# A decode block on one core: Tile's scheduling replaced by a hand-made plan of waits, Tile's closing part moved to the front, and weights kept on TensorE

## The chip, the cores and the metric

The kernel runs on one core of one Trainium2 chip. The metric is the device time of one execution in microseconds (us); less is better. Engines are named as the profile names them: PE (matmuls; PEld its weight loads), DVE, ACT, POOL, SP. SP computes nothing here; it only issues DMAs, in the order of its program, and a wait on SP holds everything behind it. All times are from one profiled execution unless another source is named.

## What is computed

One token x (1024 values) goes through a layer norm to xn. From xn come two branches, and x is added to their sum:

```python
xn = layernorm(x)
q = (xn @ wq)                       # 1024 x 4096: 32 heads of 128
k, v = last 4096 positions of the caches, 4 key heads, each shared by 8 query heads
o = softmax(q @ k.T / sqrt(128)) @ v
h = gelu(layernorm(xn) @ w1 + b1)   # 1024 x 3584
out = x + o @ wo + h @ w2 + b2      # wo 4096 x 1024, w2 3584 x 1024
```

All inputs are bf16. Nothing is used twice, so the work is reading some 40 MB from memory: K 4.2, wq 8.4, w1 7.3, V 4.2, w2 7.3, wo 8.4.

## The kernel before, in words

Everything large passes through four SBUF slots of 32 KB per partition (the ring, L63 to L68; `slots` says who lives where). Slot 0 holds K, then the second half of w1, then the first half of wo. Slot 1 holds the first half of wq, then the first half of w1, then the second half of w2. Slot 2 holds the second half of wq, then V, then the second half of wo. Slot 3 holds the transposed K as scratch (kt_scr), then the first half of w2.

SP issues the large loads in one fixed order: K in four loads, one for each key head (L75), wq in two (L94), w1 in two (L208), V in three (L214: two heads, one, one), w2 in two (L222), wo in six (L230: 16 rows at once, then 8, 4, 2, 1, 1), and at the end half of the output (L369). ACT issues the small ones: x, b2, b1 (L81 to L85), and the other half of the output (L370). A load into a slot waits until the slot's former tenant has been read: for the first half of w1 these are the matmuls of wq's first half (L239), for its second half DVE's transposes of K (L192), for V the matmuls of wq's second half, for w2's first half the copies out of kt_scr (L199, L202), for wo's second half the matmuls with V (L321).

Tile, a library, sets the semaphores: each engine's program is written in the order of the code, except where Tile's scheduler moves an instruction, and an instruction waits for those semaphores that its operands call for. At the end Tile adds a closing part: drains, barriers of all engines and the clearing of semaphores.

The stages: x is brought onto 128 partitions by eight small matmuls (L126) and normalised twice (L129 to L173), mostly on DVE, giving xnT and yT. DVE transposes K in 32 x 32 blocks (L192), and ACT (24 copies, L199) and DVE (10, L202) put the blocks in their places in kT. PE multiplies xnT with wq (L239) into eight rows, one to a column group and bank, and each matmul loads its weights again; q is transposed (L263) and put into a block matrix qm (L268); scores (L277), their maximum (L285 to L296), Exp on ACT (L299), a transpose to eTb (L301), and 32 matmuls with V into o_all (L321). In between stand the matmuls of w1 (L259) and Gelu (L314), whose result is transposed to hT (L316). Then w2's and wo's rows are summed into accf (L340), the halves of a row in two column groups in turn; x, b2 and b1 came into the sums as matmuls with one row (L181, L183, L251). The last four rows of wo (the tail, L354 to L364) go to accumulators of their own; DVE and ACT add the parts (L366, L367) and the output leaves on two queues.

Of the kernel before, what the change touches and what calls it, by code (L numbers as in the profile page):

```python
# [8 lines left out]
FP32 = mybir.dt.float32  # L9
BF16 = mybir.dt.bfloat16  # L10
ACT = mybir.ActivationFunctionType
ALU = mybir.AluOpType
AX = mybir.AxisListType


@with_exitstack
def kernel(
# [38 lines left out]
    consts = ctx.enter_context(tc.tile_pool(name="consts", bufs=1))  # L56
    small = ctx.enter_context(tc.tile_pool(name="small", bufs=2))
    ring = ctx.enter_context(tc.tile_pool(name="ring", bufs=1))
    ps_acc = ctx.enter_context(tc.tile_pool(name="ps_acc", bufs=1, space=bass.MemoryType.PSUM))
    ps_tp = ctx.enter_context(tc.tile_pool(name="ps_tp", bufs=1, space=bass.MemoryType.PSUM))  # L60
    ps_f = ctx.enter_context(tc.tile_pool(name="ps_f", bufs=2, space=bass.MemoryType.PSUM))

    RING_ELEMS = 16384  # L63

    slots = {"k_sb": 0, "wq0": 1, "wq1": 2, "kt_scr": 3, "w10": 1, "w11": 0, "v_sb": 2, "w20": 3, "w21": 1, "wo0": 0, "wo1": 2}

    def ring_tile(name):
        return ring.tile([P, RING_ELEMS], BF16, tag=f"ring{slots[name]}", name=name, align_bytes=256)  # L68

    x_flat = A_x.rearrange("a b d -> (a b d)")  # L70


    k_sb = ring_tile("k_sb")
    for g in range(Hkv):
        nc.sync.dma_start(out=k_sb[g:P - Hkv + g + 1:Hkv, :], in_=A_k_cache[0, g, Sk - W:Sk, :].rearrange("(r c) d -> r (c d)", r=P // Hkv))  # L75
    mhalf = consts.tile([P, 1], FP32)
    nc.vector.memset(mhalf[:], -0.5)
    dummy = consts.tile([1, 2], FP32)
    nc.scalar.activation(out=dummy[:, 0:1], in_=mhalf[0:1, 0:1], func=ACT.Exp)
    x_row = consts.tile([1, D], BF16)  # L80
    nc.scalar.dma_start(out=x_row[:].rearrange("a (s n) -> a s n", s=16), in_=x_flat.rearrange("(a s n) -> a s n", a=1, s=16))  # L81
    b2_row = consts.tile([1, D], BF16)
    nc.scalar.dma_start(out=b2_row[:].rearrange("a (s n) -> a s n", s=16), in_=B_b2.rearrange("(a s n) -> a s n", a=1, s=16))
    b1_row = consts.tile([1, Fd], BF16)
    nc.scalar.dma_start(out=b1_row[:].rearrange("a (s n) -> a s n", s=16), in_=B_b1.rearrange("(a s n) -> a s n", a=1, s=16))  # L85


    wq_tiles, w1_tiles = [], []
    wq_v = A_wq.rearrange("(p c) n -> p c n", p=P)
    w1_v = B_w1.rearrange("(p c) n -> p c n", p=P)  # L90
    for i in range(2):
        t = ring_tile(f"wq{i}")
        tv = t[:].rearrange("p (r n) -> p r n", r=4)
        nc.sync.dma_start(out=tv, in_=wq_v[:, 4 * i:4 * i + 4, :])  # L94
        wq_tiles.append(tv)
    kt_scr = ring_tile("kt_scr")


    ident = consts.tile([P, P], BF16)
    make_identity(nc, ident[:])  # L100
    ident_f = consts.tile([P, P], FP32)
    make_identity(nc, ident_f[:])
    ones_f = consts.tile([P, P], FP32)
    nc.vector.memset(ones_f[:], 1.0)
    sel4 = consts.tile([P, Hq], FP32)
    ones_bf = consts.tile([P, 1], BF16)
    nc.vector.memset(ones_bf[:], 1.0)
    qm = consts.tile([P, Hkv, Hq], BF16)
    nc.gpsimd.memset(qm[:], 0.0)

    spread = consts.tile([Hq, 4, P], BF16)
    nc.gpsimd.memset(spread[:], 0.0)
    nc.gpsimd.affine_select(out=spread[:], in_=spread[:], compare_op=ALU.not_equal, fill=1.0, base=0,
                            pattern=[[-1, 4], [1, P]], channel_multiplier=-4)

    gmask = consts.tile([Hq, Hkv], FP32)
    nc.gpsimd.memset(gmask[:], 1.0)
    nc.gpsimd.affine_select(out=gmask[:], in_=gmask[:], compare_op=ALU.is_ge, fill=0.0, base=0,
                            pattern=[[-REP, Hkv]], channel_multiplier=1)
    nc.gpsimd.affine_select(out=gmask[:], in_=gmask[:], compare_op=ALU.is_ge, fill=0.0, base=REP - 1,  # L120
                            pattern=[[REP, Hkv]], channel_multiplier=-1)

    xf = consts.tile([P, C], FP32)
    x_ps = ps_f.tile([P, C], FP32, tag="pf", name="x_ps")
    for c in range(C):
        nc.tensor.matmul(x_ps[:, c:c + 1], lhsT=x_row[0:1, c:D:C], rhs=ones_bf[0:1, 0:1], start=True, stop=True)  # L126
    nc.vector.tensor_copy(out=xf[:], in_=x_ps[:])

    def layernorm(src_f32, dst_f32, dst_bf):  # L129
        n = float(P * C)  # L130
        st = small.tile([P, 1], FP32, tag="ln_st")
        nc.vector.reduce_sum(out=st[:], in_=src_f32, axis=AX.X)
        tot = ps_f.tile([P, 1], FP32, tag="pf", name="ln_tot")
        nc.tensor.matmul(tot[:], lhsT=ones_f[:], rhs=st[:], start=True, stop=True)
        negmean = small.tile([P, 1], FP32, tag="ln_nm")
        nc.vector.tensor_scalar_mul(out=negmean[:], in0=tot[:], scalar1=-1.0 / n)
        xc = small.tile([P, C], FP32, tag="ln_xc")
        nc.vector.tensor_scalar(out=xc[:], in0=src_f32, scalar1=negmean[:], scalar2=None, op0=ALU.add)
        sq = small.tile([P, C], FP32, tag="ln_sq")
        st2 = small.tile([P, 1], FP32, tag="ln_st2")  # L140
        nc.vector.tensor_tensor(out=sq[:], in0=xc[:], in1=xc[:], op=ALU.mult)
        nc.vector.reduce_sum(out=st2[:], in_=sq[:], axis=AX.X)
        tot2 = ps_f.tile([P, 1], FP32, tag="pf", name="ln_tot2")
        nc.tensor.matmul(tot2[:], lhsT=ones_f[:], rhs=st2[:], start=True, stop=True)
        ve = small.tile([P, 1], FP32, tag="ln_ve")
        nc.vector.tensor_scalar(out=ve[:], in0=tot2[:], scalar1=1.0 / n, scalar2=eps, op0=ALU.mult, op1=ALU.add)
        rstd = small.tile([P, 1], FP32, tag="ln_rstd")
        nc.gpsimd.tensor_tensor(out=rstd[:], in0=ve[:], in1=mhalf[:], op=ALU.pow)
        nc.vector.tensor_scalar_mul(out=dst_f32, in0=xc[:], scalar1=rstd[:])
        nc.vector.tensor_copy(out=dst_bf, in_=dst_f32)  # L150

    xn_f = consts.tile([P, C], FP32)
    xnT = consts.tile([P, C], BF16)
    layernorm(xf[:], xn_f[:], xnT[:])
    n_el = float(P * C)
    st12 = small.tile([P, 2], FP32, tag="ln2_st")
    nc.vector.reduce_sum(out=st12[:, 0:1], in_=xn_f[:], axis=AX.X)
    sq2 = small.tile([P, C], FP32, tag="ln2_sq")
    nc.vector.tensor_tensor(out=sq2[:], in0=xn_f[:], in1=xn_f[:], op=ALU.mult)
    nc.vector.reduce_sum(out=st12[:, 1:2], in_=sq2[:], axis=AX.X)  # L160
    tot12 = ps_f.tile([P, 2], FP32, tag="pf", name="ln2_tot")
    nc.tensor.matmul(tot12[:], lhsT=ones_f[:], rhs=st12[:], start=True, stop=True)
    mean2 = small.tile([P, 1], FP32, tag="ln2_mean")
    nc.vector.tensor_scalar_mul(out=mean2[:], in0=tot12[:, 0:1], scalar1=1.0 / n_el)
    msq2 = small.tile([P, 1], FP32, tag="ln2_msq")
    nc.vector.tensor_tensor(out=msq2[:], in0=mean2[:], in1=mean2[:], op=ALU.mult)
    ve2 = small.tile([P, 1], FP32, tag="ln2_ve")
    nc.vector.tensor_scalar(out=ve2[:], in0=tot12[:, 1:2], scalar1=1.0 / n_el, scalar2=eps, op0=ALU.mult, op1=ALU.add)
    nc.vector.tensor_tensor(out=ve2[:], in0=ve2[:], in1=msq2[:], op=ALU.subtract)
    rstd2 = small.tile([P, 1], FP32, tag="ln2_rstd")  # L170
    nc.gpsimd.tensor_tensor(out=rstd2[:], in0=ve2[:], in1=mhalf[:], op=ALU.pow)
    yT = consts.tile([P, C], BF16)
    nc.vector.tensor_scalar(out=yT[:], in0=xn_f[:], scalar1=mean2[:], scalar2=rstd2[:], op0=ALU.subtract, op1=ALU.mult)  # L173

    accf = ps_acc.tile([P, 512], FP32, tag="accf")
    accq = ps_acc.tile([P, 2, 512], FP32, tag="accq", name="accq")
    nc.vector.memset(accq[:], 0.0)
    nc.vector.memset(accf[:], 0.0)
    for half in range(2):
        pr = 32 * half  # L180
        nc.tensor.matmul(accf[pr:pr + 1, :], lhsT=ones_bf[0:1, 0:1], rhs=x_row[0:1, 512 * half:512 * half + 512],  # L181
                         start=True, stop=False, tile_position=(0, pr))
        nc.tensor.matmul(accf[pr:pr + 1, :], lhsT=ones_bf[0:1, 0:1], rhs=b2_row[0:1, 512 * half:512 * half + 512],  # L183
                         start=False, stop=False, tile_position=(0, pr))


    NS = 4
# [213 lines left out]
```

## Time and profile before

| what | value |
| --- | --- |
| median of 3 runs (lowest, highest) | 102.19 us (102.12, 102.35) |
| the profiled execution | 102.22 us |
| its span, first to last instruction | 100.5 us |
| busy: PE, DVE, ACT, POOL | 48%, 46%, 32%, 4% of the span |
| weight loads on PE (beside the matmuls) | 18.7 us in 367 instructions |
| read from memory | 39.86 MB, 397 GB/s over the span |
| SP's queue q1, share of 16 DMA engines | 93.3% |

Times on lines of the profile are us from the start of the span, durations us or, where it says so, ns. The DMA row cuts the span into 40 slices of 2.5 us; each digit is the busy share of the sixteen DMA engines in tenths. The chain is followed back from the last instruction, at each step to what released it. An answer by windows gives, for each stretch, its length, the busy time of PE, PEld, DVE, ACT and POOL with the number of instructions, the granted PE clock, the DMA share and GB/s. A packet's record can fall into one slice as a whole, so single short stretches can show a share over 1.

### The profile page before, as it was taken

What the parts mean: (1) busy time and instruction counts of PE and PEld (TensorE: products, weight loads), DVE (VectorE), ACT (ScalarE), POOL (GpSimd) and SP (SyncE); (2) the same over time, 40 slices, a digit from 0 to 9 for tenths busy, and PEclk for the clock granted to TensorE, in tenths of its full rate; (3) what the DMA queues carried; (4) which work ended last, traced back from release to release, by engine and by line L of the source; (5) the groups of instructions that cost most, each with busy time, mean ns of one, the idle gap of its engine ahead of it and who ended that gap; (6) DMA issues with size and microseconds to landing.
All of it is one profiled execution on the core that took longest, in us unless ns stands there. A gap on an engine that the chain in (4) does not pass through costs nothing.

```text
span 100.5 us, 945 instructions
## 1 busy us (share of the span) xinstructions
PE 48.1 (48%) x367; PEld 18.7 (19%) x367; DVE 45.9 (46%) x64; ACT 32.1 (32%) x35; POOL 3.8 (4%) x16
## 2 busy tenths in 40 slices
PE   1565000007600930048937347991920993199780
PEld 1222000002100300024303213431400230033220
DVE  5654169999999999951234336008100000000011
ACT  4100000899999999940020472000000000000020
POOL 6033000000000000000000000000000000000000
PEclk9999999999999997555799999999997559759999
DMA  5699999999999899999999999999999999999910
GB/s 157 262 420 417 443 430 509 483 417 417 417 430 391 388 497 388 445 445 388 403 421 434 421 505 399 471 395 434 445 434 425 417 443 404 430 408 412 388 51 1
DMA packets 2494, 39.92 MB, mean 397 GB/s; under 512 B 309, under 2 KB 311, under 8 KB 698
## 3 DMA queue, kind: packets, MB, share of 16 engines
q1 hardware_dynamic: 2482, 39.85, 93.3%
q8 instruction: 3, 0.05, 0.2%
q10 hardware_dynamic: 8, 0.01, 0.0%
q14 instruction: 1, 0.01, 0.0%
HBM read 39.86 MB, written 0.00 MB: 397 GB/s over the span
## 4 chain that ended last, share of the span: by engine, by line
DMA 79%; PE 12%; SPq 5%; issue 1%; DVE 0%
DMA wq<-in_A_wq_dram 29%; DMA wo<-in_A_wo_dram 27%; DMA v_sb<-in_A_v_cache_dram 24%; PE o_all L321 7%; PE accq L239 3%; SPq L75 2%; PE acc_a L354 1%; SPq L214 1%; SPq L230 1%; SPq L94 1%; DVE res L366 0%; PE acc_b L363 0%; PE acc_b L358 0%
## 5 line engine op out<-in xcount | busy, mean ns | idle before, releaser
L199 ACT COPY kT<-kt_scr 32x1024 bf16<-32x1024 bf16 x24 | 25.0, 1042 | 15.5 <-DVE kt_scr L192 15.2
L192 DVE STREAM_TRANSPOSE kt_scr<-k_sb 128x4096 bf16<-128x4096 bf16 x4 | 17.4, 4413 | 3.1 <-DMA k_sb<-in_A_k_cache_dram 3.1
L239 PE MATMUL accq<-wq,xnT 128*1 128x512 bf16 x64 | 6.8, 601 | 20.3 <-DMA wq<-in_A_wq_dram 20.3
L202 DVE COPY kT<-kt_scr 32x4096 bf16<-32x4096 bf16 x10 | 12.2, 1219 | 0.2
L348 DVE COPY bulk_b<-accf 33x192 f32<-33x192 f32 x1 | 0.3, 350 | 25.1 <-PE accf L340 25.1
L349 ACT COPY bulk_a<-accf 33x320 f32<-33x320 f32 x1 | 0.4, 419 | 35.4 <-DVE bulk_b L348 35.4
L340 PE MATMUL accf<-w,hT 128*1 128x512 bf16 x56 | 9.0, 492 | 4.5 <-DMA w<-in_B_w_dram 4.5
L340 PE MATMUL accf<-wo,o 128*1 128x512 bf16 x56 | 7.8, 433 | 4.4 <-DMA wo<-in_A_wo_dram 4.4
L321 PE MATMUL o_all<-v_sb,eTb 128*32 128x512 bf16 x32 | 7.1, 379 | 2.1 <-DMA v_sb<-in_A_v_cache_dram 2.1
L239 PEld LDWEIGHTS <-xnT 128*1 128x1 bf16 x64 | 2.1, 116 | 24.6 <-issue 24.6
L277 PE MATMUL sp<-kT,qm 128*32 128x512 bf16 x32 | 5.6, 878 | 0.4 <-DVE qm L268 0.4
L263 PE MATMUL qT_ps<-ident,q_sb 128*128 128x128 bf16 x8 | 1.2, 308 | 8.0 <-DVE q_sb L242 8.0
L340 PEld LDWEIGHTS <-hT 128*1 128x1 bf16 x56 | 2.9, 102 | 10.1 <-issue 8.4
L340 PEld LDWEIGHTS <-o 128*1 128x1 bf16 x56 | 2.7, 92 | 9.6 <-issue 7.3
L321 PEld LDWEIGHTS <-eTb 128*32 128x32 bf16 x32 | 3.0, 97 | 6.1 <-issue 2.5
L259 PE MATMUL acch<-w,yT 128*1 128x448 bf16 x64 | 3.4, 352 | 0.0
L324 DVE TENSOR_TENSOR o_m<-o_all,grs 32x512 f32<-32x512 f32 x1 | 0.7, 678 | 5.3 <-PE o_all L321 5.3
L316 DVE STREAM_TRANSPOSE hT<-h_sb 128x896 bf16<-128x896 bf16 x1 | 1.7, 1720 | 2.4 <-ACT h_sb L314 2.4
L282 ACT COPY sc<-sp 128x512 f32<-128x512 f32 x1 | 0.6, 586 | 6.6 <-PE sp L277 6.6
L277 PEld LDWEIGHTS <-qm 128*32 128x32 bf16 x32 | 2.1, 149 | 3.1 <-issue 3.1
L280 DVE COPY sc<-sp 128x512 f32<-128x512 f32 x1 | 0.7, 692 | 3.7 <-PE sp L277 3.7
L299 ACT ACTIVATE e<-sc,nmx 128x1024 bf16<-128x1024 f32 x1 | 1.1, 1147 | 3.9 <-DVE nmx L296 3.9
(93 smaller groups left out, 38.6 us busy)
## 6 DMA issues: line engine op xcount, KB each, us to landing
w<-in_B_w_dram SPq DMA_DIRECT2D x4, 3584.0 KB, 15.7
wq<-in_A_wq_dram SPq DMA_DIRECT2D x2, 4096.0 KB
k_sb<-in_A_k_cache_dram SPq DMA_DIRECT2D x4, 1024.0 KB, 7.2
wo<-in_A_wo_dram SPq DMA_DIRECT2D x1, 4096.0 KB
v_sb<-in_A_v_cache_dram SPq DMA_DIRECT2D x1, 2048.0 KB
v_sb<-in_A_v_cache_dram SPq DMA_DIRECT2D x2, 1024.0 KB, 22.7
wo<-in_A_wo_dram SPq DMA_DIRECT2D x1, 2048.0 KB, 24.4
wo<-in_A_wo_dram SPq DMA_DIRECT2D x1, 1024.0 KB
```

The lines of the kernel that those rows point to most:

```text
L75: nc.sync.dma_start(out=k_sb[g:P - Hkv + g + 1:Hkv, :], in_=A_k_cache[0, g, Sk - W:Sk, :].rearrange("(r c) d -> r (c d)", r=P // Hkv))
L192: nc.vector.transpose(out=scr[:, s, :], in_=k2[:, s, :])
L199: nc.scalar.copy(out=kT[32 * Cd:32 * Cd + 32, R, s, :].rearrange("p (c j) -> p c j", j=32), in_=T5[32 * R:32 * R + 32, s, :, Cd, :])
L202: nc.vector.tensor_copy(out=kT[32 * Cd:32 * Cd + 32, R, :, :].rearrange("p s (c j) -> p (s c) j", j=32), in_=kt_scr[32 * R:32 * R + 32, :] ...
L239: nc.tensor.matmul(accq[32 * t:32 * t + 1, b, :], lhsT=xnT[:, c:c + 1], rhs=w3[:, r, j * 512:(j + 1) * 512], start=(c == 0), stop=(c == C ...
L259: nc.tensor.matmul(acch[32 * t:32 * t + 1, b, :NH], lhsT=yT[:, c:c + 1], rhs=w3[:, r, j * NH:(j + 1) * NH], start=False, stop=(c == C - 1) ...
L263: nc.tensor.transpose(qT_ps[:, b * 4 + hh, :], q_sb[:, b, hh * Dh:(hh + 1) * Dh], ident[:])
L277: nc.tensor.matmul(sp[32 * R:32 * R + 32, :].rearrange("p (b r u) -> p b u r", r=8, u=4), lhsT=qm[:, g, :], rhs=kv, start=(g == 0), stop=( ...
L299: nc.scalar.activation(out=e128[:], in_=sc[:], func=ACT.Exp, bias=nmx[:], scale=scale, accum_out=l_loc[:])
L316: nc.vector.transpose(out=hT[:], in_=h_sb[:].rearrange("p (d c) -> p c d", c=CW2))
L321: nc.tensor.matmul(o_all[:].rearrange("h g d -> h (g d)"), lhsT=eTb[:, 32 * c:32 * c + 32], rhs=v4[:, :, c, :], start=(c == 0), stop=(c == ...
L340: nc.tensor.matmul(accf[32 * half:32 * half + 1, :], lhsT=vec[kind](c), rhs=wap[:, half * 512:(half + 1) * 512], start=False, stop=(idx == ...
```

## The change

The kernel is written again without Tile's pools and scheduler. A class Plan collects the operations with the keys that each reads and writes, works out who must wait for whom, and writes waits and semaphores itself. Only the first two loads of K are issued inside Tile's part; then that part is closed, with its drains, barriers and clearing, and all that follows stands behind it. At the end POOL waits for the two output DMAs and clears the semaphores used.

Weights: `ldw` loads a weight and `mm` multiplies without loading, so that one load serves several matmuls. For wq and w1 a row's weight is loaded into four column groups and used for eight matmuls; for w2 it is loaded once, into the first column group, and used for both halves of the row (accumulator accw). wo keeps two column groups in turn.

Further: x is loaded as 32 rows of 32 and brought onto 128 partitions by four matmuls; b1, x and b2 are loaded across partitions (b1x, x2, b2x) after POOL has cleared those tiles and are added on DVE (xb, h_pre, base); q is transposed against a matrix of four columns; the first half of w1 is multiplied before the scores and the second half after the maximum; Gelu is one activation, with its table load placed right behind Exp; bulk_a moves from ACT to DVE. The slots, the sizes of the large loads and their order on SP are as before.

The core of the diff; the rest renames tiles and adds the keys:

```diff
-    small = ctx.enter_context(tc.tile_pool(name="small", bufs=2))
-    ring = ctx.enter_context(tc.tile_pool(name="ring", bufs=1))
-    ps_acc = ctx.enter_context(tc.tile_pool(name="ps_acc", bufs=1, space=bass.MemoryType.PSUM))
-    ps_tp = ctx.enter_context(tc.tile_pool(name="ps_tp", bufs=1, space=bass.MemoryType.PSUM))
-    ps_f = ctx.enter_context(tc.tile_pool(name="ps_f", bufs=2, space=bass.MemoryType.PSUM))
...
+class Plan:
+    def __init__(self, nc):
+        self.nc = nc
+        self.engines = {"pe": nc.tensor, "dve": nc.vector, "act": nc.scalar, "pool": nc.gpsimd, "sp": nc.sync}
+        self.ops = []
+    def add(self, eng, fn, r=(), w=(), dma=None):
+        self.ops.append((eng, fn, tuple(r), tuple(w), dma))
+
+    def emit(self, done):
+        nc, ops = self.nc, self.ops
+        writer, readers, deps = {}, {}, []
+        for n, (eng, fn, r, w, dma) in enumerate(ops):
+            need = set()
+            for k in r:
+                if k in writer:
+                    need.add((writer[k], True))
+            for k in w:
+                if k in writer:
+                    need.add((writer[k], True))
+                need.update((m, False) for m in readers.get(k, ()))
+            keep = set()
+            for m, after_write in need:
+                if m == n:
+                    continue
+                same = ops[m][0] == eng and ops[m][4] is None and dma is None
+                if same and (eng == "pe" or not after_write):
+                    continue
+                keep.add(m)
+            deps.append(keep)
+            for k in r:
+                readers.setdefault(k, []).append(n)
+            for k in w:
+                writer[k] = n
...
+        for n, (eng, fn, r, w, dma) in enumerate(ops):
+            e, lanes = self.engines[eng], {}
+            for m in waits[n]:
+                s, v = value[m]
+                if id(s) not in lanes or lanes[id(s)][1] < v:
+                    lanes[id(s)] = (s, v)
+            for s, v in lanes.values():
+                e.wait_ge(s, v)
+            i = fn()
+            if dma is not None:
+                if dma is True:
+                    dma = nc.alloc_semaphore(f"dma{n}")
+                    i.then_inc(dma, 16)
+                value[n] = (dma, 16)
+                used.append(dma)
+            elif n in wanted:
+                ticks[eng] += 1
+                i.then_inc(sems[eng], 1)
+                value[n] = (sems[eng], ticks[eng])
+        last = [value[m] for m in done]
+        for s, v in last:
+            nc.gpsimd.wait_ge(s, v)
+        nc.clear_and_free_semaphores(used)
...
-    k_sb = ring_tile("k_sb")
-    for g in range(Hkv):
-        nc.sync.dma_start(out=k_sb[g:P - Hkv + g + 1:Hkv, :], in_=A_k_cache[0, g, Sk - W:Sk, :].rearrange("(r c) d -> r (c d)", r=P // Hkv))
+    k_sem = [nc.alloc_semaphore(f"k{g}") for g in range(Hkv)]
+
+    def load_k(g):
+        return nc.sync.dma_start(out=k_sb[g:P - Hkv + g + 1:Hkv, :],
+                                 in_=A_k_cache[0, g, Sk - W:Sk, :].rearrange("(r c) d -> r (c d)", r=P // Hkv)).then_inc(k_sem[g], 16)
+
+    for g in range(2):
+        tc.no_tile_sem_insts.add(load_k(g).ins.name)
+    tc.close()
+    tc.compile()
...
+    def dma(eng, out_ap, in_ap, r=(), w=()):
+        q = plan.engines[eng]
+        plan.add(eng, lambda: q.dma_start(out=out_ap, in_=in_ap), r, w, True)
+    def ldw(w_ap, pos, r):
+        def go():
+            with nc.discard():
+                i = pe.ldweights(w_ap, tile_position=pos).ins
+            return pe.add_instruction(mybir.InstLdweights(
+                name=nc.get_next_instruction_name(), engine=i.engine, tile_size=(P, 32), tile_position=pos, ins=i.ins, outs=i.outs))
+        op("pe", go, r, ())
...
+    def mm(out_ap, w_ap, x_ap, start, stop, pos, r, w):
+        def go():
+            with nc.discard():
+                i = pe.matmul(out_ap, lhsT=w_ap, rhs=x_ap, start=start, stop=stop, tile_position=pos).ins
+            return pe.add_instruction(mybir.InstMatmult(
+                name=nc.get_next_instruction_name(), engine=i.engine, start_tensor_calc=start, stop_tensor_calc=stop,
+                tile_size=i.tile_size, tile_position=i.tile_position, ins=i.ins, outs=i.outs, ldweights=False))
+        op("pe", go, r, w)
...
+    for g in range(2):
+        plan.add("sp", lambda: None, (), (f"k{g}", "slot0"), k_sem[g])
+    for g in range(2, 4):
+        plan.add("sp", lambda g=g: load_k(g), (), (f"k{g}",), k_sem[g])
+    for i in range(2):
+        dma("sp", wq_t[i], wq_v[:, 4 * i:4 * i + 4, :], (), (f"wq{i}", f"slot{1 + i}"))
...
-    x_row = consts.tile([1, D], BF16)
-    nc.scalar.dma_start(out=x_row[:].rearrange("a (s n) -> a s n", s=16), in_=x_flat.rearrange("(a s n) -> a s n", a=1, s=16))
+    x32 = sb("x32", [Hq, Hq], BF16)
+    dma("act", x32, x_flat.rearrange("(a j) -> a j", a=Hq), (), ("x32",))
+    for name, t in (("x2", x2), ("b2x", b2x), ("b1x", b1x)):
+        op("pool", lambda t=t: pool.memset(t, 0.0), (), (name,))
+    dma("act", b1x[0:97:32, :], B_b1.rearrange("(t n) -> t n", t=4), (), ("b1x",))
+    dma("act", x2[0:33:32, :], x_flat.rearrange("(t n) -> t n", t=2), (), ("x2",))
+    dma("act", b2x[0:33:32, :], B_b2.rearrange("(t n) -> t n", t=2), (), ("b2x",))
...
+    for u in range(4):
+        mm32(x_ps, spread[:, u, :], x32[:, 8 * u:8 * u + 8], u == 0, u == 3, ("spread", "x32"), ("misc",))
...
+    xb = sb("xb", [33, 512], FP32)
+    op("dve", lambda: dve.tensor_tensor(out=xb, in0=x2, in1=b2x, op=ALU.add), ("x2", "b2x"), ("xb",))
...
-            for j in range(NJQ):
-                b, t = divmod(j, 4)
-                nc.tensor.matmul(accq[32 * t:32 * t + 1, b, :], lhsT=xnT[:, c:c + 1], rhs=w3[:, r, j * 512:(j + 1) * 512],
-                                 start=(c == 0), stop=(c == C - 1), tile_position=(0, 32 * t))
+            c = 4 * i + r
+            for t in range(4):
+                ldw(xnT[:, c:c + 1], (0, 32 * t), ("xnT",))
+            for b in range(2):
+                for t in range(4):
+                    j = 4 * b + t
+                    mm(acc2[32 * t:32 * t + 1, b, :], xnT[:, c:c + 1], wq_t[i][:, r, j * 512:(j + 1) * 512],
+                       c == 0, c == C - 1, (0, 32 * t), (f"wq{i}", f"slot{1 + i}"), ("acc2",))
+    dma("sp", w1_t[0], w1_v[:, 0:4, :], (), ("w10", "slot1"))
+    dma("sp", w1_t[1], w1_v[:, 4:8, :], (), ("w11", "slot0"))
-    v_sb = ring_tile("v_sb")
-    v4 = v_sb[:].rearrange("p (g c d) -> p g c d", g=Hkv, c=NCH)
-    for g0, g1 in ((0, 2), (2, 3), (3, 4)):
-        src = A_v_cache[0, g0:g1, Sk - W:Sk, :].rearrange("g (p c) d -> p g c d", p=P)
-        nc.sync.dma_start(out=v4[:, g0:g1, :, :], in_=src)
+    for g0, g1 in ((0, 2), (2, 3), (3, 4)):
+        dma("sp", v4[:, g0:g1, :, :], A_v_cache[0, g0:g1, Sk - W:Sk, :].rearrange("g (p c) d -> p g c d", p=P), (), (f"v{g0}", "slot2"))
...
-    for b in range(2):
-        for hh in range(4):
-            nc.tensor.transpose(qT_ps[:, b * 4 + hh, :], q_sb[:, b, hh * Dh:(hh + 1) * Dh], ident[:])
+    w1_part(0)
+            mm32(qT_ps[:, k, :], blk, selq, True, True, (f"q_sb{b}", "selq"), ("qo",))
...
+    dma("sp", slot[3][:, :14 * D].rearrange("p (r n) -> p r n", r=14), w2_v[:, 0:14, :], kt_keys, ("w20", "scr0", "scr1", "scr2", "scr3"))
+    dma("sp", slot[1][:, :14 * D].rearrange("p (r n) -> p r n", r=14), w2_v[:, 14:28, :], (), ("w21", "slot1"))
...
+    w1_part(1)
...
+    op("act", lambda: act.activation(out=dummy[:, 1:2], in_=mhalf[0:1, 0:1], func=ACT.Gelu_apprx_tanh), ("mhalf",), ("act_warm",))
...
-    for b in range(2):
-        nc.scalar.activation(out=h_sb[:, b * NH:(b + 1) * NH], in_=acch[:, b, :NH], func=ACT.Gelu_apprx_tanh, bias=zcol[:])
+    op("dve", lambda: dve.tensor_tensor(out=h_pre, in0=acc2[:, :, :NH], in1=b1x.rearrange("p (b n) -> p b n", b=2), op=ALU.add), ("acc2", "b1x"), ("h_pre",))
+    h_sb = sb("h_sb", [P, 2 * NH], BF16)
+    op("act", lambda: act.activation(out=h_sb, in_=h_pre.rearrange("p b n -> p (b n)"), func=ACT.Gelu_apprx_tanh), ("h_pre",), ("h_sb",))
...
-        for a, b in zip(cuts[:-1], cuts[1:]):
-            nc.sync.dma_start(out=tv[:, a:b, :], in_=wo_v[:, nr * i + a:nr * i + b, :])
+    wo_t = [slot[s].rearrange("p (r n) -> p r n", r=16) for s in (0, 2)]
+    dma("sp", wo_t[0], wo_v[:, 0:16, :], (), ("wo0", "slot0"))
+    cuts = [0, 8, 12, 14, 15, 16]
+    for a, b in zip(cuts[:-1], cuts[1:]):
+        dma("sp", wo_t[1][:, a:b, :], wo_v[:, 16 + a:16 + b, :], (), (f"wo1{a}", "slot2"))
...
-    for idx, (kind, c, wap) in enumerate(chunk_src[:n_bulk]):
-        for half in range(2):
-            nc.tensor.matmul(accf[32 * half:32 * half + 1, :], lhsT=vec[kind](c), rhs=wap[:, half * 512:(half + 1) * 512],
-                             start=False, stop=(idx == n_bulk - 1), tile_position=(0, 32 * half))
+    for c in range(CW2):
+        i, r = divmod(c, 14)
+        wap = slot[3 - 2 * i][:, r * D:(r + 1) * D]
+        ldw(hT[:, c, 0:1], (0, 0), ("hT",))
+        for half in range(2):
+            mm(accw[0:1, half, :], hT[:, c, 0:1], wap[:, 512 * half:512 * half + 512], c == 0, c == CW2 - 1, (0, 0), (f"w2{i}",), ("accw",))
+    for half in range(2):
+        op("dve", lambda half=half: dve.tensor_copy(out=base[32 * half:32 * half + 1, :], in_=accw[0:1, half, :]), ("accw",), ("base",))
+    op("dve", lambda: dve.tensor_tensor(out=base, in0=base, in1=xb, op=ALU.add), ("base", "xb"), ("base",))
...
+    for c in range(n_bulk):
+        wap, key = wo_row(c)
+        for half in range(2):
+            ldw(o8[:, c:c + 1], (0, 32 * half), ("o8",))
+            mm(accf[32 * half:32 * half + 1, :], o8[:, c:c + 1], wap[:, 512 * half:512 * half + 512],
+               c == 0, c == n_bulk - 1, (0, 32 * half), (key,), ("qo",))
...
-    out_v = out.rearrange("a b (t s n) -> t (a b) s n", t=2, s=16)
-    nc.sync.dma_start(out=out_v[0], in_=res[0:1, :].rearrange("a (s n) -> a s n", s=16))
-    nc.scalar.dma_start(out=out_v[1], in_=res[32:33, :].rearrange("a (s n) -> a s n", s=16))
+    out_v = out.rearrange("a b (t s n) -> t (a b) s n", t=2, s=16)
+    dma("sp", out_v[0], res[0:1, :].rearrange("a (s n) -> a s n", s=16), ("res_a", "res_b"), ("out0",))
+    dma("act", out_v[1], res[32:33, :].rearrange("a (s n) -> a s n", s=16), ("res_a", "res_b"), ("out1",))
+    plan.emit([len(plan.ops) - 2, len(plan.ops) - 1])
```

## The prediction

> **What bounds the kernel now.** I read the page's DMA row and queue table first, then the chain of work that ended last, then the timeline where that chain changes hands. The DMA row, the queue table and the head of the chain:
>
> ```profile
> DMA  5699999999999899999999999999999999999910
> ...
> q1 hardware_dynamic: 2482, 39.85, 93.3%
> ...
> DMA 79%; PE 12%; SPq 5%; issue 1%; DVE 0%
> ```
>
> SP's queue q1 carries all 39.85 MB, and from the third slice to the last but two the sixteen DMA engines are never idle. The chain in order of time says the same: its three long pieces are transfers, and what stands between them (PE L239, PE L321) only sets when SP may issue, long before the queue runs dry.
>
> ```profile
> 4.05 28.77 DMA wq<-in_A_wq_dram
> ...
> 37.08 23.69 DMA v_sb<-in_A_v_cache_dram
> ...
> 68.85 27.22 DMA wo<-in_A_wo_dram
> ```
>
> So the rule for this kernel: compute is free until it delays an issue past the point where the queue empties, and every microsecond in which q1 is empty is added to the end. The windows answer gives the full rate (last number of a row: GB/s):
>
> ```profile
> 33.00:60.80 27.80, 13.81 (x141) 5.77 (x133) 15.62 (x26) 14.96 (x17) 0.00 (x0) 0.82 1.01 431
> 60.80:92.00 31.20, 20.69 (x122) 7.78 (x124) 4.30 (x7) 0.12 (x1) 0.00 (x0) 0.84 1.00 427
> ```
>
> At that rate 1 MiB takes 2.45 us. What an empty queue costs can be read at the start, the only place where it is empty. SP issues K's first load at 0.79; nothing moves until 2.0:
>
> ```profile
> 1.50:2.00 0.50, 0.00 (x0) 0.00 (x0) 0.50 (x1) 0.50 (x1) 0.50 (x3) 1.00 0.01 4
> 2.00:2.50 0.50, 0.38 (x6) 0.39 (x7) 0.44 (x2) 0.50 (x1) 0.38 (x2) 1.00 2.98 786
> ```
>
> and in the answer for tile k_sb:
>
> ```profile
> DMA to landing us min/median/max: 5.3/7.2/9.0
> ```
>
> K's first load landed 5.3 after its issue (at 6.1), though 1 MiB needs 2.45 when it follows another: K's fourth load is in at 13.5 (DVE's first transpose starts at 13.57), so loads two to four took (13.5-6.1)/3 = 2.47 each. An empty queue cost 5.3-2.45 = 2.85. The small end: x_row, 2 KB, issued at 0.79, lets PE start at 2.11, 1.3 later; the output's 1 KB, issued at 98.41, is seen by SP at 99.69, again 1.3.
>
> **The change part by part.** One profiled execution took 102.22 (span 100.5 and 1.7 around it); the median of the three runs is 102.19, so the sum needs no correction.
>
> *SP's waits.* This decides. In the new code a DMA that writes a key already written waits for that writer, and a DMA counts as written when it has landed. The three loads of V all write "slot2", and so do the five pieces of wo's second half. The built program's list for SP confirms it: V's second and third load wait for the landing of the load before, and wo's second to fifth piece likewise; before, none of these six waited. SP works in order, so behind such a wait everything still to come is unissued: at V w2 and wo, at wo the rest of wo and the output. The queue therefore really drains, six times. Each time costs: SP wakes (0.05), issue to first data, first data's latency, last data to landing, less what a transfer in a full queue costs anyway. No row shows a drained queue in mid-kernel; from below it is 1.3 (x_row, the output: one small row each), from above 0.05+2.85 = 2.9 (K's first load). The three 1 MiB transfers (V twice, wo's second piece) are nearest to K's load, but that one ran beside the start of everything else: the trace's landing records put its first engine at 5.57, its last at 6.08, so 2.3 to 2.8 over the steady time. I take 2.4. The three small pieces (0.5, 0.25, 0.25 MiB) lie between the ends; I take 1.9. Sum 3 x 2.4 + 3 x 1.9 = **12.9**; ends 7.8 and 17.4.
>
> The Trainium skill, "DMA: Bandwidth & Descriptors", section "Anatomy of one DMA", gives a fixed cost of about 2.0 us per DMA besides bytes/436 GB/s (fitted for another issue path), nearly all of it the wait for the write's receipt. That speaks against this change: six receipts become visible, 6 x 2.0 = 12.0 as an estimate, for 114.0 in place of the total below. The rows here bracket it (1.3 and 2.85).
>
> *K.* The new program books K's first two loads as two writers of slot0, so SP also waits for the first before issuing the third. That happens at 6.1; behind it wait K's last two loads and wq. The second load is in flight until about 8.6 (6.1+2.47), and 6.15+1.3 = 7.45 brings the third's first data before that. Cover holds but barely: 0.3 (0 to 0.7).
>
> *Tile's closing part, run early.* Its drains, barriers and clearing stood between the output's landing (99.69) and the span's end (100.5), 0.8. There remain two waits on POOL and a clear; SP's like steps take 0.06 each, the clear 0.1: 0.25. **-0.55** (-0.8 to -0.3). At the front the same 0.7 comes after SP's two K issues (end 1.97), so the other engines start at 2.7, not 0.8. x then queues behind K's data: b2's row, issued at 1.40, landed at 5.9, 4.5 later, so x lands by 7.2 instead of 2.1. From xf's copy (3.75) to yT (10.5) the chain takes 6.7; with x's matmuls 0.7 and sel4 and xb ahead of the transposes (some 1.0, by L193's 0.36 and L366's 0.48) DVE starts them at 15.6 instead of 13.57. The cover: DVE's copies end at 45.4 instead of 43.4; the first w1 load, issued at 26.8, lands only at 42.5, and the second is issued when the transposes end, 33 instead of 31, so q1 stays full. eTb is ready at 60.4 instead of 58.3, and V's last load now lands at 65.6. Cost 0; were V on time at 60.8, still 0.
>
> *TensorE.* Weight loads fall from eight to four per row of wq and w1, and from two to one per row of w2; they overlap matmuls and all lie in stretches where PE waits for data afterwards (L239 idle 20.3 for wq). Worth 0. w2 now puts both halves into one column group. Before, alternate groups gave 28 matmuls in 3.19; in one group PV gives 32 in 7.07, 0.221 each. 56 x 0.221 = 12.4 in place of 9, beside 21 us of transfers of wo. Cost 0 unless the clock is at half all along (rival). w1's first half before the scores, bias and x+b2 added on DVE, one Gelu with its table load ahead: all between 45 and 75, where q1 has w2 and wo queued. 0. SP's queue order is unchanged, so no transfer is moved past another.
>
> *Tail.* From the last landing to the output's issue 1.0 as before.
>
> Sum: 102.22 + 12.9 + 0.3 - 0.55 = **114.9**.
>
> **The rivals.**
> - *Cheap restart*: all six cost 1.3, by x_row and the output: 102.22+7.8-0.55+0.3 = 109.8. For: receipt and issue are the same for any size. Against: sixteen engines must all be in, and K's load shows over 2.3.
> - *Dear restart*: 2.9 each and K 0.7: 102.22+17.4+0.7-0.55 = 119.8. Against: K's load is also the program's first.
> - *PE becomes the bound*: with the clock at 0.5 throughout w2 takes 25 us. Its second half then ends near 100 and 56 matmuls of wo (0.2 each) near 111, past wo's landing, so about 1.5 on top: 116.4. The page shows 0.5 only in three spells of some 3 to 10 us, so it is unlikely.
> - *Late front*: if the new jump after the closing part stalls SP past 6.1, K's third load comes late one for one; 1 to 2 us gives 116 to 117. For it, no row; the one jump before (to the program's body) shows no gap, 0.79 follows the barrier's release at 0.72. The Trainium skill, "Runtime: NRT & Kernel Launch", section "Instruction fetch mechanics", says that a taken branch out of the fetched window waits for a fetch; no run here shows it, and SP has 3.4 us of cover.
> - *Not slower*: DMA engines catch up after a pause, so that bytes and not the queue set the time. Place: the stretch behind each landing. Price: the waits vanish, 102.22-0.55 = 101.7. It decides from a rate behind a pause of more than twice the steady one. Against: after the cold start K ran at 2.47 per MiB, no faster than later. That the waits are not in the program is excluded by its list.
>
> **How the numbers follow.** Forecast (average restart 1.6 to 2.6) 0.62; cheap 0.15; dear 0.11; PE 0.05; late front 0.04; not slower 0.03. The range leaves out the last and the far end of dear: 109.3 to 118.5. A difference of 0.2% (102.0 to 102.4) is about what a measurement of this kernel can tell from no change; faster 0.02, same 0.01, slower 0.97.
>
> **What would show it.** In the profile after: idle slices in the DMA row near 57, 62 and four times in the last 14 us; SP waiting for DMA v_sb and wo, each wait as long as the transfer it follows; V's third load landing near 65 to 66; out issued near 111; span end 0.3 instead of 0.8 behind the output's landing; DVE's transposes at about 15.6. Wrong it would be if the DMA row stays full between 55 and 66, or if pieces of wo land 0.6 to 1.2 apart as now.

## The result and the profile after

The changed kernel takes 117.79 us (median of 4 runs, 117.57 to 118.08) against 102.2 before: a ratio of 1.1525, 95% interval 1.1496 to 1.1555. The forecast of 114.9 had the sign and the place; the time lies 2.9 above it, inside the range. In some executions the chip is in a slower state and a kernel takes over 1.5% longer than its fastest execution; those are left out of every time and ratio below.

The page of the profile after (the profiled execution took 118.08, its span is 116.3): the DMA row, SP's queue, and the chain by engine.

```profile
DMA  4998989989899999997184999989999994366320
...
q1 hardware_dynamic: 2482, 39.85, 83.0%
...
DMA 85%; PE 11%; SPq 1%; issue 0%; DVE 0%
```

The same 39.85 MB now fill 83.0% of a longer span. A slice is 2.9 us here. The row dips twice: "7184" from 52 to 64, where V is loaded, and "4366320" in the last 20 us, where wo's last pieces are. The chain in order of time (start, length, what) shows what stands there:

```profile
36.80 20.02 DMA slot<-in_A_v_cache_dram
56.82 0.02 issue
56.83 4.78 DMA slot<-in_A_v_cache_dram
61.62 0.02 issue
61.63 4.69 DMA slot<-in_A_v_cache_dram
66.32 0.04 issue
66.36 8.53 PE qo_ps L188 x32
74.89 0.02 issue
74.91 24.92 DMA slot<-in_A_wo_dram
99.83 0.02 issue
99.85 4.71 DMA slot<-in_A_wo_dram
104.56 0.02 issue
104.58 3.57 DMA slot<-in_A_wo_dram
108.14 0.02 issue
108.16 2.62 DMA slot<-in_A_wo_dram
110.78 0.02 issue
110.80 2.71 DMA slot<-in_A_wo_dram
113.51 0.04 issue
```

Each DMA row runs from the issue of a load to its landing. Where "0.02 issue" and the next DMA row follow, SP issued the next load only after that landing. Before, these loads stood in the queue one behind the other. SP's own waits say it by name (engine, line, releaser: us in total, times, longest):

```profile
SPq L174 <- DMA slot<-in_A_wo_dram: 34.5, 4, 24.6
SPq L174 <- DMA slot<-in_A_v_cache_dram: 24.1, 2, 19.6
```

Each of the six rows holds its transfer (2.45 for 1 MiB at the rate of before, 1.23 for 0.5, 0.61 for 0.25) and a gap:

| load that waited | issue to landing | transfer | gap |
| --- | --- | --- | --- |
| V, third head | 4.78 | 2.45 | 2.33 |
| V, fourth head | 4.69 | 2.45 | 2.24 |
| wo, 4 rows | 4.71 | 2.45 | 2.26 |
| wo, 2 rows | 3.57 | 1.23 | 2.34 |
| wo, 1 row | 2.62 | 0.61 | 2.01 |
| wo, last row | 2.71 | 0.61 | 2.10 |

Together 13.3, and 0.02 each for SP to wake: 13.4.

Where the whole difference of the two spans (116.3 - 100.5 = 15.8) came in can be followed along the landings (from the chains above and in the prediction, and from the trace's landing records):

| point | before | after | later by | of it new |
| --- | --- | --- | --- | --- |
| wq complete, PE goes on | 32.87 | 33.18 | 0.3 | 0.3 |
| V's first load landed | 55.89 | 56.82 | 0.9 | 0.6 |
| V complete | 60.77 | 66.32 | 5.55 | 4.6 |
| wo, first piece of the second half | 92.40 | 99.83 | 7.4 | 1.9 |
| wo complete | 97.36 | 113.51 | 16.15 | 8.7 |
| end of the span | 100.5 | 116.3 | 15.8 | -0.4 |

4.6 and 8.7 are the six gaps. The 0.3 is K's wait, the -0.4 the shorter end. What the prediction has no term for are the 0.6 and the 1.9: at these two points no transfer is new, yet the load that SP waits for is late. The DMA view of the window 97 to 99 shows one of them (forty slices of 50 ns):

```profile
DMA  7977777000000090000000000000000000000000
...
q8 instruction: 1, 0.02, 3.2%
```

The view books a packet where it starts: the last data packets start at 97.32 and take 0.61. One engine then fetches 16 KB of program code (queue q8, the lone 9 at 97.7; it takes 1.01), and SP, which waits for all sixteen engines, goes on at 99.83. In the trace's landing records fifteen engines have delivered this piece by 98.30 and the sixteenth at 99.83; V's first load likewise, 55.66 and 56.82. The packet records tie the late engine to the fetch: of the sixteen 4-byte packets that end this piece, fifteen start by 97.93 and the last at 98.74, as the fetch ends.

### The profile page after: what moved, and what is told of

It is laid out like the page before. It is cut to its first block, busy times and chain, and to the rows that moved or that the text cites. A ratio compares the mean times of both kernels' runs of the same rounds, so it can differ in the third digit from the quotient of the medians.

```text
span 116.3 us, 783 instructions
## 1 busy us (share of the span) xinstructions
PE 54.9 (47%) x351; PEld 15.3 (13%) x235; DVE 49.1 (42%) x62; ACT 31.7 (27%) x34; POOL 5.4 (5%) x19
## 3 DMA queue, kind: packets, MB, share of 16 engines
q1 hardware_dynamic: 2482, 39.85, 83.0%
## 4 chain that ended last, share of the span: by engine, by line
DMA 85%; PE 11%; SPq 1%; issue 0%; DVE 0%
DMA slot<-in_A_wo_dram 33%; DMA slot<-in_A_v_cache_dram 25%; DMA slot<-in_A_wq_dram 22%; PE qo_ps L188 7%; DMA slot<-in_A_k_cache_dram 4%; PE acc L188 3%; SPq L158 1%; SPq L174 1%; DVE res L479 0%
## 5 line engine op out<-in xcount | busy, mean ns | idle before, releaser
L304 ACT COPY kT<-slot 32x1024 bf16<-32x1024 bf16 x24 | 25.0, 1042 | 16.1 <-DVE slot L299 15.8
L299 DVE STREAM_TRANSPOSE slot<-slot 128x4096 bf16<-128x4096 bf16 x4 | 17.4, 4403 | 0.0
L188 PE MATMUL acc<-slot,xnT 128*1 128x512 bf16 x64 | 7.2, 627 | 15.8 <-DMA slot<-in_A_wq_dram 15.8
L188 PE MATMUL accw<-slot,hT 128*1 128x512 bf16 x56 | 12.4, 379 | 0.4 <-DMA slot<-in_B_w_dram 0.4
L308 DVE COPY kT<-slot 32x4096 bf16<-32x4096 bf16 x10 | 12.2, 1219 | 0.2
L188 PE MATMUL qo_ps<-slot,o 128*1 128x512 bf16 x56 | 8.1, 443 | 7.6 <-DMA slot<-in_A_wo_dram 7.6
L188 PE MATMUL acc<-slot,yT 128*1 128x448 bf16 x64 | 6.3, 574 | 10.1 <-DVE q_sb L327 10.1
L188 PE MATMUL qo_ps<-slot,eTb 128*32 128x512 bf16 x32 | 8.5, 433 | 2.8 <-DMA slot<-in_A_v_cache_dram 2.8
L188 PE MATMUL sc_ps<-kT,qm 128*32 128x512 bf16 x32 | 6.1, 980 | 0.5 <-DVE qm L356 0.5
L188 PE MATMUL acc<-slot,o 128*1 128x320 bf16 (+1 forms) x16 | 2.2, 402 | 5.6 <-DMA slot<-in_A_wo_dram 5.6
```

What stands on the lines that cost most here:

```text
L188: return pe.add_instruction(mybir.InstMatmult(name=nc.get_next_instruction_name(), engine=i.engine, start_tensor_calc=start, stop_tensor_c ...
L299: op("dve", lambda s=s: dve.transpose(out=scr[:, s, :], in_=k2[:, s, :]), ("k0", "k1", "k2", "k3", "slot0"), (f"scr{s}",))
L304: op("act", lambda s=s, R=R, Cd=Cd: act.copy(out=kT[32 * Cd:32 * Cd + 32, R, s, :].rearrange("p (c j) -> p c j", j=32), in_=T5[32 * R:32 * ...
L308: op("dve", lambda R=R, Cd=Cd: dve.tensor_copy(out=kT[32 * Cd:32 * Cd + 32, R, :, :].rearrange("p s (c j) -> p (s c) j", j=32), in_=T3[32 ...
```

## The experiments

Theory 1: the six waits on landings empty SP's queue, and that is the whole loss. Rival A: the hand-made program is slower in itself. Rival B: only the tail counts. Rival C: a wait for a landing costs its 2 us whatever is queued. Diffs are shortened. Each time below is a median; ratios are against the kernel before on the same chip.

**No wait among the pieces (e1).** The pieces behind the first no longer write the slot's key.

```diff
-    plan.add("sp", lambda: None, (), (f"k{g}", "slot0"), k_sem[g])
+    plan.add("sp", lambda: None, (), (f"k{g}", "slot0") if g == 0 else (f"k{g}",), k_sem[g])
...
-... (), (f"v{g0}", "slot2"))
+... (), (f"v{g0}", "slot2") if g0 == 0 else (f"v{g0}",))
...
-... (), (f"wo1{a}", "slot2"))
+... (), (f"wo1{a}", "slot2") if a == 0 else (f"wo1{a}",))
```

> The changed kernel with only the keys altered: V's second and third load, wo's second to fifth piece and K's second load no longer write the slot's key, so SP waits for no landing among them; all else is as changed. Theory 1 (the queue runs dry six times, 13.4 us of gaps in the profile, and the slowest DMA engine is waited for at two more places, some 1.7): 117.8 - 13.4 - 1.7 - 0.3 (K) = 102.4, with 0.6 either way; the DMA row is full from 2 to 97. Rival A (the hand-made order itself is slower: late front, w2 in one column group, own waits on compute): at least 107, with the gain of the waits taken up by other idle time.

Measured 102.34 (102.12 to 102.56), ratio 1.0011, interval 0.9997 to 1.0024. All 15.45 us are gone with the seven waits, and the rest of the rewriting, front to end, adds up to nothing that can be measured. It is a balance: wo is complete at 97.72 against 97.36 before, and the end behind it is about as much shorter. Rival A falls. The DMA row of its page:

```profile
DMA  3799999999999999998899998998999999999920
```

**V's waits away, wo's kept (e2), and the reverse (e3).** The edits are the second and the third of e1, each alone.

> Only V's two waits taken away; wo's four and K's one stay. Theory 1: two gaps of 2.35 and 2.25 go, and of the slowest engine's lag at V 0.3 to 1.1: 112.1 to 112.9, four gaps left in the last 14 us. Rival B (what matters is the tail alone, since V's gaps are made up later under the long transfers of w2 and wo): 117.0 to 117.8. Rival A: no row of the changed profile gives V less than its gaps, but below 1 us of gain would fit it.

Measured 110.69 (110.56 to 110.72), ratio 1.0815, interval 1.0792 to 1.0839: 7.1 gained, 1.4 more than theory 1 allowed.

> Only wo's four waits taken away; V's two and K's one stay. Theory 1: gaps of 2.27, 2.35, 2.03 and 2.1 go, 8.75 in all, and up to 0.4 of the engine's lag: 108.6 to 109.1; this and the run without V's waits should add up to the run without any. Rival B: 102 to 103, as the tail is everything. Rival A: above 112.

Measured 108.99 (108.48 to 109.83), ratio 1.0661, interval 1.0608 to 1.0714: 8.8 gained, as expected. Rival B falls with both. Together the two gain 15.9, where the run without any wait gains 15.45 with K's wait gone as well, so they do not add up as exactly as expected.

The miss of e2 is instructive. Measured from e1, wo's four waits and K's cost 110.69 - 102.34 = 8.35; the gaps in e2's chain are

```profile
93.05 4.44 DMA slot<-in_A_wo_dram
...
97.50 3.51 DMA slot<-in_A_wo_dram
...
101.03 2.46 DMA slot<-in_A_wo_dram
...
103.50 2.64 DMA slot<-in_A_wo_dram
```

1.99 + 2.28 + 1.85 + 2.03 = 8.15, and with 0.2 for K (below) that is 8.35. But V's two waits and K's cost 108.99 - 102.34 = 6.65, where e3's chain has gaps of only 2.36 and 2.32:

```profile
56.51 4.81 DMA slot<-in_A_v_cache_dram
...
61.33 4.77 DMA slot<-in_A_v_cache_dram
```

1.8 is left over. In the landing records of every kernel on the new plan the last DMA engine is 1.1 to 1.8 behind the median of the sixteen at V's first load, after a code fetch at 49.8 to 53.8, and in most of them one falls behind again late in the run. The kernel before fetches at 37.55, and there the lag stands already at the first load of w1, 1.64, where the others have 0.3 to 0.7. The packet records show its size: each fetch takes 0.9 to 1.1, and where it meets a full queue, a data packet that starts just as it ends takes some 0.5 longer than its like (in the changed kernel, at 51.15, 0.86 instead of 0.31 for 8 KB): some 1.5 in all.

Without waits such lags lie side by side on different engines, and the end pays the largest once (1.4 in e1's landing records). A wait for a landing in the middle pays it there, starts all engines level, and the end pays the next one: in e3 1.59 at V and 1.56 at the end, in e2 1.58 once. So V's waits cost their gaps and one lag more.

**Waits kept, but with something queued behind (e4).** The two loads of w2 go between V's three.

```diff
     load_v(0, 2)
+    dma("sp", slot[3]... w2_v[:, 0:14, :] ...)
     load_v(2, 3)
+    dma("sp", slot[1]... w2_v[:, 14:28, :] ...)
     load_v(3, 4)
```

> All waits stay, but on SP the two loads of w2 are put between V's three: while SP waits for a landing, 3.7 MB are still queued. Theory 1 (a wait costs only because the queue runs dry): V's two gaps vanish although the waits are there, 112 to 113.5; V's last load lands near 78 instead of 66, PV ends near 86, still before wo's first half is in (88), and PE ends w2 near 100, about 108 for wo, close to the transfers. Rival C (each wait for a receipt costs its 2 us whatever is queued): 117.8.

Measured 112.77 (112.68 and 112.86), ratio 1.1022, interval 1.0991 to 1.1054, as theory 1 expected. SP waits for V as often as in the changed kernel, but the DMA row no longer dips there. Its waits, then the row:

```profile
SPq L174 <- DMA slot<-in_A_v_cache_dram: 19.5, 2, 10.2
```

```profile
DMA  3998999999989999999999999999999495815330
```

Two waits of up to 10.2 us left no gap, because 3.7 MB were queued behind each awaited load: V's three landings (56.28, 67.27, 78.26) lie 10.99 apart, what the 4.72 MB between two of them take at 430 GB/s. Rival C falls. The 5.0 gained are the two gaps of 4.6 and little more; e2, without these waits, is another 2.1 faster. V is complete only at 78.3 here and PE becomes the bound: from there to the end the chain holds no transfer, and PE's rows fill it but for some 2.5 us on DVE.

```profile
78.31 8.43 PE qo_ps L188 x32
...
89.05 11.53 PE accw L188 x53
...
101.23 5.54 PE qo_ps L188 x52
```

**Only K's wait (e5).** e1 without its first edit.

> The kernel without the six waits (102.34), but with K's wait kept: SP issues K's third load only when the first has landed. Theory 1 (the second load covers it but for a few tenths; in the changed profile K was complete 0.42 later than before): 102.5 to 102.8. Rival C (each wait costs its 2 us): 104.3. Rival: no cost at all, 102.3.

Measured 102.55 (102.33 to 102.73), ratio 1.0026, interval 1.0010 to 1.0042. 0.2 more than e1, at the lower end, with intervals that overlap; in the landing records wq is complete at 33.04 against 32.73 in e1. The second load of K covers most of the wait for the first.

**The closing ahead of all loads (e6).**

```diff
-    for g in range(2):
-        tc.no_tile_sem_insts.add(load_k(g).ins.name)
     tc.close()
...
+    for g in range(4):
+        plan.add("sp", lambda g=g: load_k(g), ...)
```

> The kernel without the six waits and without K's, with Tile's part closed before any load is issued, so that K's loads stand behind the closing's drains, barriers and clearing. If the early closing is harmless only because two loads go ahead of it: K starts later by the closing's own time on SP (two barrier rounds, 0.5 to 0.8), and so does everything: 102.8 to 103.2. If the front is hidden in any case: 102.3. If the closing waits for more than itself: above 103.5.

Measured 102.93 (102.80 to 103.03), ratio 1.0057, interval 1.0039 to 1.0075. K's first load is issued at 1.45 instead of 0.80, and 0.6 us later everything ends. So the early closing is free only because two loads go ahead of it.

**Weights loaded for every matmul again (e7).** `ldw` issues nothing and `mm` is an ordinary matmul.

> The kernel without the six waits and without K's, with a weight load for every matmul again, as before the change (351 weight loads instead of 235); the same sums. Theory: PE waits for data in every stage, so 102.1 to 102.6, no difference. Rival: repeated loads lengthen the last stretch behind wo's landing and fetch more program code: 102.8 to 103.8.

Measured 102.4 (102.28 to 102.64), ratio 1.0015, interval 0.9999 to 1.0032: the same as e1, with 351 weight loads against 235 in the profiles. Not repeating them is worth nothing here.

**Two waits more (e8).** wo's second half in pieces of 4, 4, 2, 2, 2, 1, 1 rows.

```diff
-    cuts = [0, 8, 12, 14, 15, 16]
+    cuts = [0, 4, 8, 10, 12, 14, 15, 16]
```

> The changed kernel with wo's second half cut into seven pieces instead of five (4, 4, 2, 2, 2, 1, 1 rows), each still waiting for the one before: the same bytes, the same work on PE, two waits more, on pieces of 0.5 and 0.25 MiB. Theory 1 (a dry queue costs 2.0 to 2.35 whatever the size): 117.8 + 4.0 to 4.7 = 121.8 to 122.5. Rival D (the cost goes with the bytes that stand behind the wait, as the 1 MiB pieces' share of the gaps would have it): under 120. Rival B (pieces are late for PE, not for the queue): 117.8.

Four rows are 1 MiB, not 0.5 as the expectation has it: the two added gaps stand before pieces of 1 and 0.5 MiB. Measured 120.98 (120.4 to 121.53), ratio 1.1824, interval 1.1758 to 1.1891: 3.2 more than the changed kernel, 0.8 below the least expected. The gaps are all there:

```profile
95.71 4.85 DMA slot<-in_A_wo_dram
100.58 3.53 DMA slot<-in_A_wo_dram
...
104.13 3.48 DMA slot<-in_A_wo_dram
...
107.62 3.47 DMA slot<-in_A_wo_dram
...
111.11 2.60 DMA slot<-in_A_wo_dram
...
113.72 2.68 DMA slot<-in_A_wo_dram
```

2.40, 2.30, 2.25, 2.24, 1.99, 2.07: 13.25 against 8.7 in the changed kernel, 4.5 more. The profiled executions differ by 2.9 (120.98 and 118.08), and the missing 1.6 is the lag again: here the late code fetch (95.15) fell into a gap, and the first piece's sixteenth engine landed 0.3 behind the median instead of 1.85. From 1 MiB to 0.25 MiB, a quarter of the bytes, the gap falls from 2.4 to 2.0: rival D, cost by bytes, falls.

**K's second load on ACT's queue (e9).** From e1, for a better start than both kernels have.

```diff
-        return nc.sync.dma_start(out=k_sb[...],
+        return (nc.scalar if g == 1 else nc.sync).dma_start(out=k_sb[...],
```

> The kernel without the six waits and without K's, with K's second load issued by ACT ahead of the closing instead of by SP, so that two queues are filled at 0.8 instead of one. If the dry queue at the start costs partly because a single queue ramps up (in the profile of the kernel without waits the first 32 KB packets take longer than later ones): 101.9 to 102.2, better than both kernels. If it is latency alone, which a second queue cannot shorten: 102.3. If two queues get in each other's way, or x behind K on ACT's queue comes too late: 102.6 or more.

Measured 102.45 (102.35 to 102.86), ratio 1.0012, interval 0.9997 to 1.0026: no difference, K is complete at 13.3 in both, so a second queue does not shorten the start. What the Trainium skill says in "DMA: Bandwidth & Descriptors", section "Issuing engines are not separate DMA queues", that DMAs of several issuing engines run on the same sixteen DMA engines and save only issue time, agrees with it.

## Why the prediction was right, and where it was short

- *SP's six waits.* Right in mechanism and nearly in size: 12.9 forecast, 13.4 found. The 2.4 for the large pieces were 2.2 to 2.3; the 1.9 for the small ones, taken between a tiny row's 1.3 and K's first load, were 2.0 to 2.3. So a tiny row, at 1.3, was a poor lower end for a piece spread over sixteen engines. The Trainium skill's fixed cost of about 2.0 per DMA ("DMA: Bandwidth & Descriptors", "Anatomy of one DMA"), fitted there for another issue path, would have given 12.0 as an estimate. The gaps here, 2.0 to 2.3, lie a little above it.
- *The missing term.* "Less what a transfer in a full queue costs anyway" took the sixteen engines as level. They are not: one lags 1.1 to 1.8, and each stage with waits pays such a lag anew. The changed kernel pays 1.83 at V and 1.85 at wo's first piece, the kernel before 1.53 once, at its end: 2.15 of the 0.6 + 1.9 = 2.5 in the table. The rest stands at V, where the median engine, too, is 0.65 later, of which K's wait explains 0.3. The same account can be held against e1, which pays 1.42 once: 13.4 of gaps, 2.3 of lag and K's 0.3 make 16.0, and the profiled executions differ by 15.8 (118.08 and 102.25). That the time lies in the range is in part luck: the range's upper part was made for dearer restarts, which did not come, and for the lag it had nothing. The Trainium skill, "DMA: Bandwidth & Descriptors", section "Why a DMA increments its semaphore by 16 and not by 1", says that only the full count of 16 means that all data have landed. The landing records above agree: SP's wait lasts to the sixteenth engine, at 99.83. That the code fetch makes the lag is read from the packet records and from its time in all eleven profiles; no run took a fetch away to show it.
- *K's wait*, 0.3: 0.2 to 0.3 (e5, first landing row).
- *The closing*, -0.55 at the end: -0.4. At the front the loads ahead of it were the cover, and without them it costs 0.6 (e6).
- *The late front.* DVE's transposes were forecast at 15.6 and start at 16.25, in e1 even at 17.26, and cost nothing there (e1 is level with before). The jump behind the closing stalls nobody: that rival did not come.
- *TensorE.* w2 in one column group takes 12.4 as worked out and costs nothing; the weight loads are worth nothing (e7). PE as the bound appeared only in e4, where V came 12 us later still.
- *Cheap and dear restart.* Neither: in all runs together the gaps lie between 1.85 and 2.65, so they reach neither 1.3 nor 2.9. Nor did the engines catch up behind a pause (*not slower*): the first packets there were slower than later ones (last section).

## What to carry to other kernels

In a kernel whose time is its transfers, look in the built program for every wait on the issuing engine and ask what is still queued when it ends: with megabytes behind it a wait of 10 us left no gap, with nothing behind it each cost some 2.2 us (1.85 to 2.65) for pieces of 0.25 to 1 MiB. A dependency tracker that names whole buffers, as this one did, makes such waits by itself between loads that fill parts of one buffer; one key for each part, with the former tenant's key on the first part only, took 15 us away here. And a wait for a landing waits for the slowest of sixteen engines, so two such stages pay two lags.

## What the runs showed that was not expected

- Fetching program code costs a DMA engine time in a full queue: 0.9 to 1.1 us for 16 KB in the packet records, and some 0.5 for the data packet behind it. After it one engine was 1.1 to 1.8 behind the median and stayed so as long as the queue was full; at e1's end the lag was still 1.4.
- Mid-kernel, the first packet started 0.95 after SP's issue (99.85 to 100.80 in the packet records of the changed kernel), against 1.3 for the program's first load. The first packets were slow in both places: 0.4 to 1.1 for 8 KB instead of 0.31, and 1.3 to 2.2 for 32 KB at the start instead of 1.2. The gap was 2.26 against 2.75 for K's first load in the same run.
